# Moving the operand tiles of two expert layers to other bytes of their partitions, in a long convolution followed by two expert layers

## The chip, the cores and the metric

The kernel runs on one core of one Trainium2 chip. The metric is the device time in microseconds of one execution; the time before is the median of three. All rows below are from one profiled execution of the kernel before the change.

## The reference

Three stages follow one another: a gated long convolution done with Fourier transforms, then two expert layers (matrices 128 x 2048 and 2048 x 128), on 24,960 tokens of width 128.

```python
def _attn_ref(x, v, pos_emb, w1, w2):
    ...
    u = x * v
    ...
    y = np.fft.irfft(Uf * Hf[None, :, :], n=L, axis=1)[:, :S, :]
    return (x * y).astype(np.float32)

def _moe_ref(x, w_in, w_out):
    h = x @ w_in
    g = h * np.cos(h)
    return (g @ w_out).astype(np.float32)

def _moe2_ref(x, w_in, w_out):
    h = x @ w_in
    relu6 = np.clip(h + 3.0, 0.0, 6.0)
    g = h * relu6 / 6.0
    return (g @ w_out).astype(np.float32)
```

## The kernel before, in words

Every engine's program is written out in a fixed order; no scheduler decides it. The convolution (function `conv_phase`) comes first. While it runs, the weights of both experts are decoded into SBUF (`decode`), each matrix as a pair of tiles of type fp32r: a high part (`w_hi`) and a low part (`w_lo`). The names in the profile are `wi` and `wo` for the in and out matrices of the first expert, `vi` and `vo` for those of the second.

Then `moe_phase` runs both experts over tiles of tokens: 49 tiles, of which the first and the last have 448 tokens and the others 512. A tile of the first expert is `xh` and `xl` (high and low part of the input; for the first tile of all `x0h` and `x0l`), of the second expert `x2h` and `x2l`. Each tile is worked through in 8 units. A unit has a front (L696) of six matmuls with 128 x 128 weights and 512 (or 448) moving columns, two blocks of three: high weights with high input, high weights with low input, low weights with high input. It writes PSUM tile `ha` (first expert, in the main part) or `hb` (second expert). ScalarE, VectorE and GpSimd then make the gated value and its split `hi` and `lo`. A unit's back (L764) is six more matmuls: `hi` twice on the high weights, `hi` twice on the low weights, `lo` twice on the high weights, into PSUM tile `acc`.

In the main part one pass of the loop over `p` issues on TensorE, in this order, the front of a unit of the first expert (`ha<-xh,wi`), the back of an earlier one (`acc<-hi,wo`), the front of a unit of the second expert (`hb<-x2h,vi`, 12 units behind), and the back of an earlier one of those (`acc<-hi,vo`): 24 matmuls. Passes 0 to 11 hold units of the first expert alone, the last 12 those of the second alone, and 380 passes in between hold both. Each matmul has its own weight load (PEld in the profile), which runs while the matmul before it is still streaming.

**Where the tiles lie.** The tile pools are stacked in each partition from byte 0 up, each tile padded to a multiple of 32 bytes. Sizes are fixed, so the first byte of each tile follows from adding them up. What matters here is that byte modulo 256. All tiles of a pool of `moe_phase` are multiples of 2048 bytes, every weight block is 512 bytes from the next, the low part of a weight tile 8192 from the high part, and the second half of `hi` and `lo` 2048 from the first, so that one number holds for all matmuls of a kind. Before the change:

| tiles | first byte modulo 256 |
|---|---|
| `wi`, `wo` (weights, first expert) | 128 |
| `vi` (weights in, second expert) | 160 |
| `vo` (weights out, second expert) | 192 |
| `x0h`, `x0l` (moving, first tile) | 128 |
| `xh`, `xl`, `x2h`, `x2l`, `hi`, `lo` (moving) | 224 |

Three sizes make the odd places: tile `x0` has 4 x 113 x 4 = 1808 bytes (16 over a multiple of 256, padded to 32), and `vi` and `vo` share their memory with the filter tiles `h0` and `h1` of the convolution, 36 x 114 x 4 = 16,416 bytes each (32 over). Below, "offset" is the first byte of the moving tile less that of the weights, modulo 256: 96 with `wi` and `wo`, 64 with `vi`, 32 with `vo`, 0 for `x0h` and `x0l` with `wi`.

Of the kernel before, what the change touches and what calls it, by code (L numbers as in the profile page):

```python
# [9 lines left out]
FP32 = mybir.dt.float32  # L10
F32R = mybir.dt.float32r
# [12 lines left out]
N1, N2 = 111, 113  # L24
# [4 lines left out]
MP = 2 * M2  # L29
# [4 lines left out]
DFF = 2048  # L34
KFF = DFF // 128
TOK = B * S
TT = 512
XW = 4 * N2
TILES = [(TT + TOK % TT) // 2] + [TT] * (TOK // TT - 1) + [(TT + TOK % TT) // 2]
TWO_PI = 2.0 * np.pi  # L40

# [2 lines left out]
def kernel(  # L44
# [19 lines left out]
    nc = tc.nc  # L64
    dram = ctx.enter_context(tc.tile_pool(name="dram", bufs=1, space=DRAM))
    wp = ctx.enter_context(tc.tile_pool(name="wp", bufs=1))
    scr = dram.tile([D, B, NP1 * N2], FP32, name="scr")
# [5 lines left out]
    hq = ctx.enter_context(tc.tile_pool(name="hq", bufs=1))  # L73

    def weights(e, nm):
        if (nm, e) not in w_hi:
            if e == 0:
                t = wp.tile([128, 2, DFF], F32R, name=f"w{nm}")
            else:
                t = hq.tile([128, 2, DFF], F32R, tag=f"h{'io'.index(nm)}", name=f"v{nm}")  # L80
            w_hi[nm, e], w_lo[nm, e] = t[:, 0, :], t[:, 1, :]
        return w_hi[nm, e], w_lo[nm, e]

# [23 lines left out]
    def decode(task, st, pool, lane):  # L107
        e, nm, c = task
        lo, hi = st[:, :, 0], st[:, :, 1]
        ex = pool.tile([128, DC], INT32, tag=f"wex{lane}", name="wex")  # L110
        mh = pool.tile([128, DC], INT32, tag=f"wmh{lane}", name="wmh")
        m = mh.bitcast(FP32)
        wh, wl = (w[:, c:c + DC] for w in weights(e, nm))
        nc.vector.tensor_scalar(ex, hi, 9, 0x3FFFFF, op0=ALU.logical_shift_right, op1=ALU.bitwise_and)
        nc.vector.tensor_scalar(mh, hi, 0x1FF, None, op0=ALU.bitwise_and)
        yield
        nc.scalar.activation(out=ex, in_=ex, func=ACTF.Relu, bias=b_exp, scale=-1.0)
        nc.scalar.activation(out=ex, in_=ex, func=ACTF.Relu, bias=b_max, scale=-(2.0 ** 12))
        nc.scalar.activation(out=m, in_=mh, func=ACTF.Copy, scale=2.0 ** -20)
        yield  # L120
        nc.vector.scalar_tensor_tensor(
            out=ex, in0=hi, scalar=-0x80000000, in1=ex, op0=ALU.bitwise_and, op1=ALU.bitwise_or
        )
        yield
        nc.scalar.copy(wh, ex.bitcast(FP32))
        nc.vector.scalar_tensor_tensor(
            out=m, in0=lo.bitcast(UINT32), scalar=2.0 ** -52, in1=m, op0=ALU.mult, op1=ALU.add
        )
        yield
        nc.vector.tensor_scalar(ex, ex, -0x800000, None, op0=ALU.bitwise_and)  # L130
        yield
        nc.gpsimd.tensor_tensor(out=wl, in0=m, in1=ex.bitcast(FP32), op=ALU.mult)
# [17 lines left out]
    x0_t = {}  # L150
    x0h = wp.tile([128, TILES[0]], F32R, name="x0h")
    x0l = wp.tile([128, TILES[0]], F32R, name="x0l")

    def conv_phase(cctx):
# [408 lines left out]
            mk_y(i)  # L563

        n = NG
        x0 = x0_t[0] = wp.tile([128, XW], FP32, name="x0")

        def x_tile(shape, name):
            return p_x.tile(shape, FP32, tag="x", name=name)
# [8 lines left out]
        v = ps_v.tile([NP1, 2, 512], FP32, tag="v", name="v")  # L578
# [9 lines left out]
        def pass_on(i, z, eng, cs_=range(CH)):  # L588
            for c in cs_:
                d = i * CH + c  # L590
                eng.dma_start(
                    out=x0[d:d + 1, :].rearrange("c (n m) -> c n m", m=N2), in_=z[:XW // N2, 0, c, :N2]
                )

        s1i_3(0)
# [13 lines left out]
        w_of(n - 1, 0, wp_)  # L609
        fin_of(n - 1, 0, z1[:, 0], nc.vector, wp_[:, 1])  # L610
        e = (n - 3) * CH
        nc.sync.dma_start(out=x0[:e], in_=scr[:e, 0, :XW])
        pass_on(n - 3, z3, nc.sync)
        pass_on(n - 2, z2, nc.sync, (0,))
        pass_on(n - 1, z1, nc.sync)
        s1i_3(1)
        s2i(n - 2, 1)
# [10 lines left out]
                store_of(i, b, z[:, b])  # L628

    def moe_phase(mctx):  # L630
        x_p = mctx.enter_context(tc.tile_pool(name="x_p", bufs=3))
        x2_p = mctx.enter_context(tc.tile_pool(name="x2_p", bufs=2))
        o_p = mctx.enter_context(tc.tile_pool(name="o_p", bufs=2))
# [6 lines left out]
        nc.scalar.activation(out=dummy, in_=bias3, func=ACTF.Sin)  # L640
        NT = len(TILES)
        starts = [sum(TILES[:t]) for t in range(NT)]
        xs = {}
# [3 lines left out]
        def n_of(t):  # L647
            return TILES[t]

        def load_x(t):  # L650
            if t >= NT:
                return
            n = n_of(t)
            if t == 0 and n <= XW and _runs(0, n) == [[0, 0, n]]:
                xf[t] = x0_t[t]
# [135 lines left out]
        for p in range(P2 + 3):  # L791
            if p < P1:
                t, u = divmod(p, NU)
# [36 lines left out]
    with tc.manual_schedule():  # L830
        nc.gpsimd.memset(b_exp, 1151.0 * 2.0 ** 11 - 1.0)
        nc.gpsimd.memset(b_max, 255.0 * 2.0 ** 23 - 2.0 ** 12)
        nc.gpsimd.memset(b_one, 1.0)
        nc.gpsimd.memset(bias3, 3.0)
        nc.gpsimd.memset(biaspi, float(np.pi / 2))
        nc.gpsimd.memset(biasq, 0.25)
        with ExitStack() as cctx:
            conv_phase(cctx)
        with ExitStack() as mctx:
            moe_phase(mctx)  # L840
# [8 lines left out]
def _runs(a, n):  # L849
    valid = np.flatnonzero(_order()[1].reshape(-1) < S)  # L850
    runs = []
    for j in range(a, a + n):
        b, p = j // S, int(valid[j % S])
        if runs and runs[-1][0] == b and runs[-1][1] + runs[-1][2] == p:
            runs[-1][2] += 1
        else:
            runs.append([b, p, 1])
    return runs
# [78 lines left out]
```

## Time and profile before

| | us |
|---|---|
| time before, median of 3 (lowest, highest) | 2731.19 (2731.03, 2733.28) |
| span of the profiled execution | 2729.6 |
| convolution, to the last of its matmuls | about 529 |
| start of the experts, with waits, to 591 us | about 62 |
| the 376 passes in which both experts have fronts and backs, from 591 us | about 2096 |
| last passes and store | about 42 |
| PE busy in the span | 2712.7 (99%) |
| DVE, ACT, POOL busy | 2343.9, 2184.7, 2410.3 (86%, 80%, 88%) |

The profiled execution's own time is its span of 2729.6 us, 1.6 us under the median: what lies around the span is within the spread of the times. Matmuls in the profile overlap (the recorded length of one is near 0.39 us while the next starts 0.23 us later), so a busy PE tells little, and what counts is the distance from one matmul's start to the next one's, called the pitch below. A merged row of a timeline ends its stretch where the last matmul of the row ends, so pitches are taken from the starts of rows and the counts between them.

### The profile page before, as it was taken

What the parts mean: (1) busy time and instruction counts of PE and PEld (TensorE: products, weight loads), DVE (VectorE), ACT (ScalarE), POOL (GpSimd) and SP (SyncE); (2) the same over time, 40 slices, a digit from 0 to 9 for tenths busy, and PEclk for the clock granted to TensorE, in tenths of its full rate; (3) what the DMA queues carried; (4) which work ended last, traced back from release to release, by engine and by line L of the source; (5) the groups of instructions that cost most, each with busy time, mean ns of one, the idle gap of its engine ahead of it and who ended that gap; (6) DMA issues with size and microseconds to landing.
All of it is one profiled execution on the core that took longest, in us unless ns stands there. A gap on an engine that the chain in (4) does not pass through costs nothing.

```text
span 2729.6 us, 45722 instructions
## 1 busy us (share of the span) xinstructions
PE 2712.7 (99%) x16362; PEld 2151.5 (79%) x16362; DVE 2343.9 (86%) x3188; ACT 2184.7 (80%) x3140; POOL 2410.3 (88%) x1321
## 2 busy tenths in 40 slices
PE   9999999999999999999999999999999999999999
PEld 6777777678888888888888888888888888888888
DVE  7999998788888888888888888888888888888887
ACT  5666665588888888888888888888888888888885
POOL 6999998689888888888888989888988888888987
PEclk9999999999999999999999999999999999999999
DMA  4334333200000000000000000000000000000000
GB/s 122 100 105 106 105 98 83 64 5 16 8 16 8 16 9 16 9 16 9 16 8 16 13 11 16 9 16 9 16 9 16 8 16 8 16 9 16 8 8 12
DMA packets 88312, 79.86 MB, mean 29 GB/s; under 512 B 57028, under 2 KB 78870, under 8 KB 88086
## 3 DMA queue, kind: packets, MB, share of 16 engines
q1 hardware_dynamic: 87790, 76.80, 10.4%
q8 instruction: 132, 2.16, 0.3%
q14 instruction: 94, 0.77, 0.1%
q10 hardware_dynamic: 296, 0.13, 0.0%
HBM read 51.15 MB, written 25.74 MB: 28 GB/s over the span
## 4 chain that ended last, share of the span: by engine, by line
PE 98%; ACT 1%; DVE 1%; POOL 0%; issue 0%; DMA 0%; SPq 0%; ACTq 0%; DVEq 0%
PE acc L764 40%; PE hb L696 20%; PE ha L696 19%; PE ap L277 5%; PE v L277 3%; PE xp L277 3%; PE bp L277 3%; PE xh L277 2%; PE ap L276 1%; PE rp L329 0%; PE hps L342 0%; PE bp L276 0%; ACT r L716 0%; POOL lo L729 0%; ACT k L706 0%
## 5 line engine op out<-in xcount | busy, mean ns | idle before, releaser
L754 POOL TENSOR_TENSOR lo<-g,hi 128x1024 fp32r<-128x1024 f32 (+1 forms) x390 | 939.2, 2408 | 237.7 <-PE ha L696 157.1
L729 POOL TENSOR_TENSOR lo<-g,hi 128x1024 fp32r<-128x1024 f32 (+1 forms) x392 | 942.6, 2405 | 3.5 <-ACT hi L724 2.8
L706 ACT ACTIVATE k<-ha,biasq 128x512 int32<-128x512 f32 (+1 forms) x768 | 509.0, 689 | 293.7 <-PE ha L696 293.6
L717 DVE TENSOR_TENSOR g<-ha,r 128x512 f32<-128x512 f32 (+1 forms) x768 | 500.0, 690 | 283.8 <-ACT r L716 283.7
L696 PE MATMUL hb<-x2h,vi 128*128 128x512 f32 (+1 forms) x1564 | 549.8, 392 | 0.0
L696 PE MATMUL ha<-xh,wi 128*128 128x512 f32 (+1 forms) x1524 | 535.1, 391 | 3.1 <-DVE g L717 3.1
L716 ACT ACTIVATE r<-r,biaspi 128x512 f32<-128x512 f32 (+1 forms) x776 | 520.0, 719 | 0.4 <-DVE r L707 0.4
L707 DVE SCALAR_TENSOR_TENSOR r<-k,ha 128x512 f32<-128x512 int32 (+1 forms) x768 | 488.9, 677 | 2.9 <-ACT k L706 2.3
L737 DVE SCALAR_TENSOR_TENSOR g<-q,hb 128x1024 f32<-128x1024 f32 (+1 forms) x391 | 472.7, 1209 | 8.3 <-ACT q L736 8.2
L751 DVE SCALAR_TENSOR_TENSOR hi<-q,hb 128x1024 fp32r<-128x1024 f32 (+1 forms) x390 | 470.1, 1205 | 0.0
L736 ACT ACTIVATE q<-hb,bias 128x1024 f32<-128x1024 f32 (+1 forms) x391 | 435.3, 1113 | 20.8 <-PE hb L696 17.4
L764 PE MATMUL acc<-hi,wo 128*128 128x512 f32 (+1 forms) x1568 | 428.6, 395 | 0.0
L764 PE MATMUL acc<-hi,vo 128*128 128x512 f32 (+1 forms) x1568 | 428.2, 395 | 0.0
L724 ACT CAST hi<-g 128x1024 fp32r<-128x1024 f32 (+1 forms) x385 | 399.7, 1038 | 0.0
L764 PEld LDWEIGHTS acc<-hi,wo 128*128 128x128 f32 x1568 | 295.5, 188 | 71.5
L696 PEld LDWEIGHTS hb<-x2h,vi 128*128 128x128 f32 x1564 | 293.9, 188 | 69.0 <-issue 0.4
L764 PEld LDWEIGHTS acc<-hi,vo 128*128 128x128 f32 x1568 | 294.3, 188 | 68.5
L696 PEld LDWEIGHTS ha<-xh,wi 128*128 128x128 f32 x1524 | 286.0, 188 | 71.0 <-issue 2.8
L696 PE MATMUL hb<-x2l,vi 128*128 128x512 f32 (+1 forms) x782 | 306.5, 392 | 0.0
L696 PE MATMUL ha<-xl,wi 128*128 128x512 f32 (+1 forms) x762 | 303.7, 399 | 0.0
L764 PE MATMUL acc<-lo,wo 128*128 128x512 f32 (+1 forms) x784 | 248.0, 397 | 0.5 <-POOL lo L729 0.2
L764 PE MATMUL acc<-lo,vo 128*128 128x512 f32 (+1 forms) x784 | 245.8, 394 | 0.0
(155 smaller groups left out, 4084.1 us busy)
## 6 DMA issues: line engine op xcount, KB each, us to landing
x<-in_x_dram SPq DMA_DIRECT2D x64, 199.5 KB
v<-in_v_dram SPq DMA_DIRECT2D x64, 199.5 KB
scr<-z SPq DMA_DIRECT2D x128, 98.9 KB
out_dram<-o SPq DMA_DIRECT2D x47, 256.0 KB
xf<-scr SPq DMA_DIRECT2D x17, 256.0 KB
wst<-in_wi_dram SPq DMA_DIRECT2D x8, 512.0 KB
wst<-in_wo_dram SPq DMA_DIRECT2D x8, 512.0 KB
pt<-in_post_dram SPq DMA_DIRECT2D x14, 224.0 KB
```

Of the source, the lines that this page charges most:

```text
L277: nc.tensor.matmul(out=out[OD:m], lhsT=lhsT[:, OD:m], rhs=rhs if rhs2 is None else rhs2)
L696: nc.tensor.matmul(out=hs[c][:, 0, :n], lhsT=w["i", e][:, sl], rhs=r[:, :n], start=(k == 0), stop=(k == 2))
L706: nc.scalar.activation(out=k[:, c, :n], in_=h, func=ACTF.Identity, bias=biasq, scale=1.0 / TWO_PI)
L707: nc.vector.scalar_tensor_tensor(out=un.r[:, c, :n], in0=k[:, c, :n], scalar=-TWO_PI, in1=h, op0=ALU.mult, op1=ALU.add)
L716: nc.scalar.activation(out=rc, in_=rc, func=ACTF.Sin, bias=biaspi, scale=1.0)
L717: nc.vector.tensor_tensor(out=un.g[:, c, :n], in0=h, in1=rc, op=ALU.mult)
L729: nc.gpsimd.tensor_tensor(out=un.lo[:, :, :n], in0=un.g[:, :, :n], in1=un.hi[:, :, :n], op=ALU.subtract)
L736: nc.scalar.activation(out=un.r[:, c, :n], in_=h, func=ACTF.Relu, bias=bias3, scale=1.0)
L737: nc.vector.scalar_tensor_tensor(out=un.g[:, c, :n], in0=un.r[:, c, :n], scalar=6.0, in1=h, op0=ALU.min, op1=ALU.mult)
L751: nc.vector.scalar_tensor_tensor(out=un.hi[:, c, :n], in0=un.r[:, c, :n], scalar=6.0, in1=h, op0=ALU.min, op1=ALU.mult)
L754: nc.gpsimd.tensor_tensor(out=un.lo[:, :, :n], in0=un.g[:, :, :n], in1=un.hi[:, :, :n], op=ALU.subtract)
L764: nc.tensor.matmul(out=acc[e][:, :n], lhsT=w["o", e][:, sl], rhs=r[:, c, :n], start=(u == 0 and c == 0 and k == 0), stop=(u == KFF // 2 - ...
```

## The change

The sizes of five tiles are rounded up to a multiple of 256 bytes, and a tile of 64 bytes that nothing uses is put ahead of the pools of `moe_phase`. All weights then start at byte 128 modulo 256, and all moving tiles from the second on at byte 192: the offset is 64 in every front and back. `x0h` and `x0l` stay at 128, offset 0. Every tile of the convolution that lies above `x0` moves up as well, those above `h0` and `h1` all by the same 672 bytes, so that the offsets among them stay what they were. No instruction is added, removed, resized or put elsewhere in its engine's order, and every wait waits for the same semaphore and count as before.

```diff
+LINE = 64
+HB = -(-max(36 * MP, 2 * DFF) // LINE) * LINE
+XB = -(-XW // LINE) * LINE
...
-                t = hq.tile([128, 2, DFF], F32R, tag=f"h{'io'.index(nm)}", name=f"v{nm}")
+                t = hq.tile([128, HB], F32R, tag=f"h{'io'.index(nm)}", name=f"v{nm}")[:, :2 * DFF]
+                t = t.rearrange("p (z f) -> p z f", f=DFF)
...
-        x0 = x0_t[0] = wp.tile([128, XW], FP32, name="x0")
+        x0 = x0_t[0] = wp.tile([128, XB], FP32, name="x0")
...
-                    out=x0[d:d + 1, :].rearrange("c (n m) -> c n m", m=N2), in_=z[:XW // N2, 0, c, :N2]
+                    out=x0[d:d + 1, :XW].rearrange("c (n m) -> c n m", m=N2), in_=z[:XW // N2, 0, c, :N2]
...
-        nc.sync.dma_start(out=x0[:e], in_=scr[:e, 0, :XW])
+        nc.sync.dma_start(out=x0[:e, :XW], in_=scr[:e, 0, :XW])
...
     def moe_phase(mctx):
+        step = mctx.enter_context(tc.tile_pool(name="step", bufs=1))
+        step.tile([128, LINE // 4], FP32, name="step")
```

## Rows read from the trace of the kernel before

**Rows 1.** The page: span, busy time, and the chain that ended last.
```profile
span 2729.6 us, 45722 instructions
PE 2712.7 (99%) x16362; PEld 2151.5 (79%) x16362; DVE 2343.9 (86%) x3188; ACT 2184.7 (80%) x3140; POOL 2410.3 (88%) x1321
...
PE 98%; ACT 1%; DVE 1%; POOL 0%; issue 0%; DMA 0%; SPq 0%; ACTq 0%; DVEq 0%
PE acc L764 40%; PE hb L696 20%; PE ha L696 19%; PE ap L277 5%; PE v L277 3%; PE xp L277 3%; PE bp L277 3%; PE xh L277 2%; PE ap L276 1%; PE rp L329 0%; PE hps L342 0%; PE bp L276 0%; ACT r L716 0%; POOL lo L729 0%; ACT k L706 0%
```

**Rows 2.** Busy time of each engine by stage: busy us and count, granted clock.
```profile
core 0: us, PE busy (x) PEld busy (x) DVE busy (x) ACT busy (x) POOL busy (x), PEclk, DMA share, GB/s
0.00:528.70 528.70, 524.48 (x6936) 382.14 (x6938) 454.48 (x796) 323.09 (x655) 463.93 (x474) 1.00 0.37 98
528.70:591.00 62.30, 53.14 (x225) 42.56 (x222) 45.97 (x60) 50.09 (x68) 53.10 (x36) 0.95 0.11 30
...
633.80:2644.90 2011.10, 2011.10 (x8641) 1621.38 (x8640) 1739.96 (x2206) 1721.68 (x2295) 1788.85 (x766) 1.00 0.04 12
2644.90:2687.40 42.50, 42.50 (x194) 36.06 (x193) 36.98 (x50) 35.25 (x52) 36.61 (x17) 1.00 0.02 7
2687.40:2729.60 42.20, 38.71 (x181) 33.33 (x179) 29.64 (x30) 17.09 (x21) 30.42 (x15) 0.99 0.03 13
```

**Rows 3.** Timeline of the weight loads in one front and back.
```profile
642.17 0.19 PEld L696 LDWEIGHTS hb<-x2l,vi 128*128 128x128 f32 x1
```

**Rows 4.** Timeline of PE in one pass of the main part.
```profile
639.37 0.39 PE L696 MATMUL ha<-xh,wi 128*128 128x512 f32 x1
639.60 0.40 PE L696 MATMUL ha<-xl,wi 128*128 128x512 f32 x1
639.84 0.62 PE L696 MATMUL ha<-xh,wi 128*128 128x512 f32 x2
...
642.17 0.40 PE L696 MATMUL hb<-x2h,vi 128*128 128x512 f32 x1
642.41 0.39 PE L696 MATMUL hb<-x2l,vi 128*128 128x512 f32 x1
642.64 0.62 PE L696 MATMUL hb<-x2h,vi 128*128 128x512 f32 x2
643.10 0.39 PE L696 MATMUL hb<-x2l,vi 128*128 128x512 f32 x1
643.32 0.39 PE L696 MATMUL hb<-x2h,vi 128*128 128x512 f32 x1
643.55 1.10 PE L764 MATMUL acc<-hi,vo 128*128 128x512 f32 x4
```

**Rows 5.** Chain that ended last, in time order: start, us, what; first passes.
```profile
617.52 1.41 PE ha L696 x6
618.93 1.40 PE acc L764 x6
620.33 1.37 PE hb L696 x6
621.70 1.24 PE acc L764 x6
...
639.53 1.39 PE ha L696 x6
640.93 1.40 PE acc L764 x6
642.33 1.39 PE hb L696 x6
643.72 1.40 PE acc L764 x6
```

**Rows 6.** Timeline of PE while the granted clock was 0.50, and the clock.
```profile
575.25:577.30 2.05, 2.05 (x6) 1.63 (x5) 2.00 (x3) 2.02 (x4) 2.05 (x2) 0.50 0.01 4
575.63 1.91 PE L764 MATMUL acc<-hi,wo 128*128 128x512 f32 x4
577.34 1.00 PE L764 MATMUL acc<-lo,wo 128*128 128x512 f32 x2
```

**Rows 7.** Timeline of PE with 448 columns: convolution, first tile, last tile.
```profile
206.58 0.54 PE L277 MATMUL xp<-at,cs 121*49 121x448 f32 x1
206.96 0.54 PE L277 MATMUL xp<-at,cs 121*49 121x448 f32 x1
...
536.70 0.36 PE L696 MATMUL hb<-x0h,wi 128*128 128x448 f32 x1
538.92 0.37 PE L696 MATMUL hb<-x0h,wi 128*128 128x448 f32 x1
...
2714.91 0.37 PE L696 MATMUL hb<-x2h,vi 128*128 128x448 f32 x1
2716.12 0.98 PE L764 MATMUL acc<-hi,vo 128*128 128x448 f32 x4
2717.35 0.36 PE L696 MATMUL hb<-x2h,vi 128*128 128x448 f32 x1
```

**Rows 8.** Timeline of DVE, and of PE, around the release of `ha`.
```profile
1503.59 1.30 DVE L717 TENSOR_TENSOR g<-ha,r 128x512 f32<-128x512 f32 x2 [0.23 <-ACT r L716]
...
1505.77 0.62 PE L696 MATMUL ha<-xh,wi 128*128 128x512 f32 x2
```

## The prediction

> **What bounds the kernel now.** First the page: the chain that ended last lies 98% on PE, and four fifths of it are the fronts and backs of the two experts, L696 and L764 [rows 1]. Then the busy times by stage: from 633.80 to 2644.90 us PE has no gap at all, at a granted clock of 1.00 (the level of 2.4 GHz), while DVE, ACT and POOL are busy for 1740, 1722 and 1789 of 2011.10 us [rows 2]. These are 360 passes of 24 matmuls, 8640 (the row counts 8640 loads), so a pass takes 5.586 us and the mean pitch is 232.8 ns. The time is set by how fast PE goes from one matmul to the next, and by nothing that PE waits for.
>
> Now what such a pitch should be. 512 columns at 2.4 GHz are 213.3 ns, so each of these matmuls loses about 19 ns. At the lower level nothing is lost: where the granted clock was 0.50, four matmuls took 1.71 us from start to start, 427 ns each, and 512 columns at 1.2 GHz are 426.7 [rows 6]. The convolution loses little at 2.4 GHz: its matmuls of 448 columns, which go through their columns twice, have a pitch of 0.38 us, 190 ns or less for once, against 186.7 worked out and against 202 to 205 ns for the experts' matmuls of 448 columns [rows 7]. So some 18 ns per matmul are lost in the experts alone and at the full clock alone. Under every matmul the weight load for the next one is running: the load of `hb<-x2l,vi` starts at 642.17, as the matmul before it does [rows 3, 4].
>
> **Does the loss depend on where the tiles lie?** Within a pass the pitches are uneven, though all 24 matmuls have the same shape: the front of the second expert has steps of 0.24, 0.23, 0.46 for two, 0.22 and 0.23 us [rows 4]. Sorted by the offset of the weights that load meanwhile:
>
> - Offset 96 (`wi`, `wo`): six take 1.39 to 1.41 us, 232 to 235 ns each [rows 5].
> - Offset 32 (`vo`), 512 columns: 1.40 us for six, 233 ns [rows 5].
> - Offset 64 (`vi`): 1.39 in the main part, but 1.37 in the first passes, 228 ns [rows 5]. In the main part it begins with the slow step of 0.24 and ends with faster ones, 0.91 us for the last four [rows 4]: what a matmul costs depends also on the steps before it, and six matmuls are few to settle in. In the passes around 620 us it has settled from its first step on.
> - With 448 columns the same: offset 64 takes 1.21 us for six (201.7 ns) and offset 32 takes 1.23 (205 ns), in neighbouring rows; offset 0 (`x0h` on `wi`) takes 2.22 us for eleven, 201.8 ns [rows 7].
>
> So offsets 0 and 64 are alike, 32 and 96 are alike, and the first pair is 3 to 5 ns cheaper per matmul. As far as these rows go, whole multiples of 64 bytes are good and odd multiples of 32 are bad.
>
> The Trainium skill speaks against any such effect: its page "TensorE: Matmul & The Clock Gate", in the section on what each phase is for, says that TensorE reads the moving operand and the weights through two independent SBUF ports, so that loading the next weights takes no read bandwidth from the running matmul. By that rule the change is worth nothing and the time stays at 2731; the pitches that differ by weight tile do not fit it.
>
> **The change part by part.** No instruction, size, order or wait changes, so there is no added work to price. Four things move.
>
> *Fronts and backs with 512 columns.* All now stand at offset 64, with no step from one offset to another within a pass or between passes. I price each six at the settled 1.37 us of the vi front [rows 5]. A pass becomes 4 x 1.37 = 5.48 us, 0.106 less than 5.586, and 360 passes give -38 us. The row is rounded to 0.01: half a hundredth on each six is 7 us on 360 passes. Bounds: from above the worst six with the same shape, 1.41 (a loss, below); from below the rate of the convolution, at most 190 ns for 448 columns, thus 215 ns or so for 512 and 1.29 for six. I stay with 1.37, since it is the one row with the very offset, columns and type.
>
> *Passes with 448 columns in one expert.* There are 8 at each end, the last 8 taking 42.50 us [rows 2]. A six at 448 gains about 0.02 where it had offset 32 or 96 [rows 7] and one at 512 gains 0.026 as above, some 0.1 a pass: -1.5 us. The last twelve passes hold `vo` backs beside `vi` fronts: -0.3. The start of the experts has 9 us without a matmul in 62 [rows 2] and offset 0 in its fronts, and I count nothing there.
>
> *The convolution.* Its tiles move together, so their offsets stay. Its pitch is at the bound already, so there is nothing to gain. If the place alone, without the offset, brought in the experts' loss of 8%, its 524 us of PE would cost 42 more; no row suggests it, and I take 0.
>
> *The elementwise engines.* They read and write the moved tiles, and no pitch of PE follows them. A faster PE asks more of them: per pass POOL has 1788.85 / 360 = 4.97 us of work, DVE 4.83, ACT 4.78, against a new 5.48 [rows 2]. The tightest loop that I see is PSUM tile `ha`: its last reader on DVE ends at 1504.89, and the first matmul that overwrites this half is the second of the pair that starts at 1505.77, thus at 1506.00 [rows 8]. That leaves 1.1 us of cover, and a pass shorter by 0.1 uses a tenth of it. If the cover were gone, PE would wait and the gain would end where POOL's 4.97 stand, beyond my forecast.
>
> Sum: -38 - 1.5 - 0.3 = -40, with 2 us less because the 1.37 contains one step towards another offset, and because a row of 1.37 may stand for up to 1.375: I take -39. The profiled execution (span 2729.6) is 1.6 us under the median, so I take the difference off the median: 2731.2 - 39 = 2692.
>
> **Rivals.**
>
> *It doesn't settle.* The cheap run at 620 us may hang on the state that it was entered from, and the main part's vi front (1.39) may be what offset 64 gives on the whole. Then a pass is 4 x 1.39 = 5.56, 0.026 less, and 376 passes give -10: 2721; with 1.385, inside that row's rounding, 2714. For it: the slow first step of every vi front in the main part. Against it: by their last steps these fronts do 0.91 for four. Chance 0.14.
>
> *Nothing changes.* The uneven steps come from the order of the matmuls and not from the place of the weights, and the time stays at 2731. For it: fronts at offset 96 also show 1.39 in the main part. Against it: the rows with 448 columns, where the order is the same in both experts. Chance 0.08. (It is what the rule of the Trainium skill named above would give.)
>
> *Slower, by the place and not the offset.* The vi front is the only one of the 512-column rows in which both streams start at an odd multiple of 32 (160 and 224), and after the change both start at an even one (128 and 192). If that costs what the worst front costs, 1.41 for six, a pass takes 5.64: +0.054 x 360 = +19, so 2751. It decides from a mean six of about 1.400 on. Against it: `x0h` and `wi` both start at 128 and go at 201.8 ns, among the best with 448 columns [rows 7]. Chance 0.06, the convolution's 42 us included.
>
> *More than forecast.* If every step were the best single one, 0.225, a pass would be 5.40, and -0.186 x 360 = -67 gives 2664; at the convolution's rate it would be near 2580. A front that already has offset 64 shows neither. Chance 0.12, nearly all of it above 2660.
>
> **How the numbers follow.** The forecast (2684 to 2703 by its own rounding and transitions) has 0.60. With "doesn't settle" at 0.14 and half of "more" the range is 2668 to 2722, which leaves out no change, slower and the far end of more: 0.2. A change of 0.2%, 5.5 us, is about what a measurement of this kernel can tell from none; "doesn't settle" lies beyond it for all but 0.02. So faster 0.84, same 0.10, slower 0.06.
>
> **What would show it.** Right: in the main part the stage of 360 passes lasts about 1973 us instead of 2011.10, all four sixes of a pass read 1.37, PE still has no gap, the convolution's 528.7 us stay, and the durations of the elementwise operations stay. Wrong: sixes of 1.39 or 1.40 in spite of offset 64 everywhere (no settling, or no effect of the offset), a six over 1.40 (the place matters), or waits of PE on `g` or `lo` in the main part (an elementwise engine has become the bound).

## The result and the profile after

The changed kernel takes 2696.1 us (median of 4, 2695.94 to 2697.06), 0.9872 of the time before, with a 95% interval of 0.9858 to 0.9886. The forecast was 2692 in 2668 to 2722, faster. The profiled execution's span is 2694.4 us, 35.2 less than that of before.

Busy times by stage, of the changed kernel; columns as in [rows 2], which answers row by row, but for the third row here, the first passes with both experts; its row of before stands below:

```profile
0.00:528.70 528.70, 523.89 (x6928) 380.76 (x6930) 453.97 (x794) 322.38 (x654) 463.79 (x474) 1.00 0.37 98
528.70:591.26 62.56, 54.16 (x234) 43.02 (x233) 46.59 (x63) 51.08 (x69) 53.72 (x37) 0.95 0.11 31
591.26:633.37 42.11, 42.11 (x193) 36.01 (x192) 36.74 (x49) 37.42 (x52) 37.34 (x17) 1.00 0.04 13
633.37:2610.97 1977.60, 1977.60 (x8642) 1622.61 (x8640) 1739.63 (x2206) 1705.11 (x2296) 1782.97 (x766) 1.00 0.05 13
2610.97:2652.66 41.69, 41.69 (x193) 36.03 (x192) 36.82 (x50) 35.02 (x52) 36.52 (x17) 1.00 0.02 7
2652.66:2694.40 41.74, 38.27 (x181) 33.29 (x179) 29.60 (x30) 17.16 (x22) 30.57 (x15) 0.99 0.04 13
```

Before the change:

```profile
590.97:633.78 42.81, 42.81 (x193) 36.07 (x192) 36.82 (x49) 37.56 (x52) 37.41 (x17) 1.00 0.04 12
```

The 360 full passes take 1977.60 us instead of 2011.10: -33.5 of the 35.2. The 8 passes with 448 columns at each end give 0.7 and 0.8, the last twelve 0.5, and convolution and start of the experts together end 0.3 later. PE still has no gap in the passes. In time order the chain of the changed kernel reads, where [rows 5] had 1.39 and 1.40:

```profile
639.03 1.37 PE ha L702 x6
640.40 1.37 PE acc L770 x6
641.77 1.37 PE hb L702 x6
643.15 1.37 PE acc L770 x6
```

and the timeline of PE, where [rows 4] began the `vi` front with a step of 0.24 us:

```profile
641.61 0.39 PE L702 MATMUL hb<-x2h,vi 128*128 128x512 f32 x1
641.84 0.39 PE L702 MATMUL hb<-x2l,vi 128*128 128x512 f32 x1
642.07 0.62 PE L702 MATMUL hb<-x2h,vi 128*128 128x512 f32 x2
642.52 0.39 PE L702 MATMUL hb<-x2l,vi 128*128 128x512 f32 x1
642.75 0.39 PE L702 MATMUL hb<-x2h,vi 128*128 128x512 f32 x1
642.99 1.07 PE L770 MATMUL acc<-hi,vo 128*128 128x512 f32 x4
```

Every step is now 0.22 to 0.24. The starts in nanoseconds show one cycle of three, 226, 229 and 231 or 232, in all four sixes: 5493 or 5494 ns in each of the 361 passes with 512 columns alone. That is the run that the `vi` front showed around 620 us before the change.

### The profile page after: what moved, and what is told of

Its sections match the earlier page's. It is cut to its first block, busy times and chain, and to the rows that moved or that the text cites. A ratio compares the mean times of both kernels' runs of the same rounds, so it can differ in the third digit from the quotient of the medians.

```text
span 2694.4 us, 45722 instructions
## 1 busy us (share of the span) xinstructions
PE 2677.7 (99%) x16362; PEld 2151.7 (80%) x16362; DVE 2343.4 (87%) x3188; ACT 2168.2 (80%) x3140; POOL 2404.9 (89%) x1321
## 4 chain that ended last, share of the span: by engine, by line
PE 98%; POOL 1%; ACT 1%; DVE 1%; issue 0%; DMA 0%; ACTq 0%; DVEq 0%; POOLq 0%
PE acc L770 39%; PE hb L702 20%; PE ha L702 19%; PE ap L281 5%; PE v L281 3%; PE xp L281 3%; PE bp L281 3%; PE xh L281 2%; PE ap L280 1%; PE rp L333 1%; PE hps L346 0%; PE bp L280 0%; POOL lo L735 0%; ACT k L712 0%; ACT r L722 0%
## 5 line engine op out<-in xcount | busy, mean ns | idle before, releaser
L770 PE MATMUL acc<-hi,wo 128*128 128x512 f32 (+1 forms) x1568 | 420.1, 390 | 0.0
L770 PE MATMUL acc<-hi,vo 128*128 128x512 f32 (+1 forms) x1568 | 419.5, 389 | 0.0
```

Of the source, the lines that this page charges most:

```text
L770: nc.tensor.matmul(out=acc[e][:, :n], lhsT=w["o", e][:, sl], rhs=r[:, c, :n], start=(u == 0 and c == 0 and k == 0), stop=(u == KFF // 2 - ...
```

## The experiments

Each run edits the changed kernel, unless it says otherwise. "Offset" is still the moving tile's first byte less that of the weights, modulo 256.

**1. Many offsets, by extra matmuls.** Sets of 40 matmuls stand behind the twelve matmuls `busy<-wi` that the kernel issues ahead of the experts, with a narrow one ahead of each set. The granted clock was 1.00 over all sets. The added work counts in its time, 3460.92 us, so only the pitches are read.

```diff
+        wa, wb = w_hi["i", 0], w_hi["o", 0]
+        scan = [(0, k, 128, TT) for k in range(64)]
+        scan += [(0, k, m, TT) for m in (64, 32) for k in (0, 8, 16, 24)]
+        scan += [(j, j + 16, 128, TT) for j in (4, 8, 12)] + [(j, j + 24, 128, TT) for j in (4, 8, 12)]
+        scan += [(0, k, 128, 448) for k in (0, 8, 16, 24)]
+        for j, k, m, n in scan:
+            nc.tensor.matmul(out=busy[:32, :64], lhsT=wb[:, :32], rhs=wb[:, :64])
+            for _ in range(40):
+                nc.tensor.matmul(out=busy[:m, :n], lhsT=wa[:, j:j + m], rhs=wa[:, k:k + n])
```

> The changed kernel with 82 sets of 40 extra matmuls (128 x 128 weights unless said otherwise, 512 columns) behind the twelve that warm TensorE; they read two slices of the first expert's weights and write a PSUM tile that nothing reads. In a set all matmuls have one offset between moving slice and weights; sets step it by 4 bytes from 0 to 252. Theory A (the offset modulo 64 counts): the pitch repeats every 64 bytes, lowest at 0, 64, 128, 192 (about 227 to 229 ns) and high at 32, 96, 160, 224 (about 233). Theory B (64 itself counts): a lowest pitch near 64 alone. Theory C (only that the offset is the same everywhere counts): all sets alike, about 228.6. Loads of 64 and 32 columns: if the loss comes from the load that runs under a matmul, it falls from some 15 to 20 ns over 213.3 in proportion to the columns loaded; if it is a fixed cost of a matmul it stays. Sets that shift weights and moving slice together by 16, 32, 48 bytes: the same pitch if the offset alone counts, another if the place does.

Timeline of PE in that run, sets with offsets 0, 32, 64 and 100, each with the narrow matmul that ends it:

```profile
533.16 9.36 PE L802 MATMUL busy<-wi 128*128 128x512 f32 x40
542.36 0.19 PE L800 MATMUL busy<-wo 128*32 128x64 f32 x1
...
608.25 9.58 PE L802 MATMUL busy<-wi 128*128 128x512 f32 x40
617.66 0.19 PE L800 MATMUL busy<-wo 128*32 128x64 f32 x1
...
683.31 9.42 PE L802 MATMUL busy<-wi 128*128 128x512 f32 x40
692.57 0.19 PE L800 MATMUL busy<-wo 128*32 128x64 f32 x1
...
768.13 9.82 PE L802 MATMUL busy<-wi 128*128 128x512 f32 x40
777.79 0.19 PE L800 MATMUL busy<-wo 128*32 128x64 f32 x1
```

The 40 take 9.20, 9.41, 9.26 and 9.66 us. Without the first step of each set (some 0.31 us, behind the narrow matmul) and the steps until the set has settled, the mean distance of starts over the last 29 is:

```
offset (bytes)          0     32     64     96    128    160    192    224
pitch, 512 cols (ns)  226.7  233.4  228.8  233.4  232.3  234.2  233.2  233.4
lowest and highest of all 64 offsets: 226.7 (0, 28, 60, 108, 156, 252) and 240.0 (68, 100, 132, 180, 196, 228, 244)
weights of 64 columns 230.1  230.8  228.4  230.1
weights of 32 columns 231.6  233.3  231.6  233.3
448 moving columns    206.7  200.0  200.0  205.3
```

Theory A is wrong: 128 and 192 are multiples of 64 and cost about as much as 32. Theory C is wrong: a set has one offset and still pays 226.7 to 240. Theory B holds no better, as 0 beats 64. The loss does not shrink in proportion to the columns loaded: at offsets 32 and 96 a load of 64 columns costs about 3 ns less, but one of 32 columns no less, and at offset 0 the narrower load costs more. With 448 columns the order of the offsets is another one. The sets that shift weights and moving slice together show that the place can count besides the offset: offset 64 costs 226.7 ns with a shift of 16 or 48 bytes, against 228.8 with 0 or 32; offset 96 stays at 233.3 to 233.4.

**2. Offset 0 in the whole kernel.** The 64-byte tile is taken out, the rounded sizes stay.

```diff
-        step = mctx.enter_context(tc.tile_pool(name="step", bufs=1))
-        step.tile([128, LINE // 4], FP32, name="step")
```

> The changed kernel without the 64-byte tile: all moving tiles of the experts start where the weights do, modulo 256 (offset 0). Theory A (offset modulo 64): as the changed kernel or a little faster, sixes of 1.36 to 1.37 us, 2685 to 2697 us. Theory B (64 itself): slower than the changed kernel, sixes of 1.39 to 1.41, 2715 to 2745. Theory C (uniformity): 2696.

It takes 2677.39 us, 0.9801 of before (0.9787 to 0.9816), with sixes of 1.36. That is below what any of the three theories gave (2685 at the least), and it is the scan's price for offset 0: 24 x 226.7 ns are a pass of 5.440 us, which the trace shows. So the rounding of sizes alone gains 54 us, and the 64-byte tile then gives back 19 of them. It is the fastest kernel of this study.

**3. Offset 96.**

```diff
-        step.tile([128, LINE // 4], FP32, name="step")
+        step.tile([128, 3 * LINE // 8], FP32, name="step")
```

> The changed kernel with a tile of 96 bytes in place of 64: offset 96 in every front and back. Theory A (offset modulo 64): the gain is lost or more than lost; all sixes at the 1.40 of the wo backs before, a pass of 5.60 us, about 2735 us. Theory B: above 2715 as well. Theory C (uniformity alone): 2696, with sixes of 1.37.

2736.93 us, 1.0018 of before (1.0009 to 1.0028): one offset everywhere gains nothing if it is this one. Uniformity is not the cause. Theory A had this time too (2735), so this run alone does not tell it from a price for each offset; runs 1 and 10 do.

**4. Another place, the same offset.**

```diff
     dummy = wp.tile([128, 1], FP32, name="dummy")
+    wp.tile([128, 8], FP32, name="place")
```

> The changed kernel with a 32-byte tile ahead of all tiles of the experts: the offset stays 64 everywhere, but weights start at 160 and moving tiles at 224 modulo 256, as the second expert's front did before. Theories A, B and C (offset or uniformity): 2696, sixes of 1.37. Theory D (both streams have to start at a multiple of 64): the gain is lost wholly or in part, above 2710.

2696.35 us, 0.987 (0.9854 to 0.9886), as the changed kernel. Where both streams lie does not count, for this offset and a shift of 32 bytes.

Busy times over one and the same stretch show what a uniform offset costs, since PE has no gap in it; four of them: the changed kernel (64),

```profile
640.00:2600.00 1960.00, 1960.00 (x8565) 1608.16 (x8564) 1724.22 (x2187) 1690.66 (x2276) 1767.48 (x759) 1.00 0.05 12
```

offset 0,

```profile
640.00:2600.00 1960.00, 1960.00 (x8650) 1623.16 (x8649) 1742.07 (x2208) 1701.03 (x2299) 1778.70 (x766) 1.00 0.05 13
```

offset 96,

```profile
640.00:2600.00 1960.00, 1960.00 (x8402) 1576.75 (x8401) 1691.24 (x2145) 1676.47 (x2231) 1743.51 (x744) 1.00 0.05 12
```

and offset 68, run 8 below:

```profile
640.00:2600.00 1960.00, 1960.00 (x8168) 1568.03 (x8167) 1677.65 (x2085) 1634.50 (x2171) 1408.05 (x724) 1.00 0.04 12
```

The stretch divided by the count is the pitch: 228.8, 226.6, 233.3 and 240.0 ns, at a granted clock of 1.00 in all four. These are the prices of the first scan, to 0.1 ns.

**5. More sets: farther away, fewer columns, other reads.**

```diff
+        for k in (256, 264, 281, 512, 520, 537, 1024, 1032, 1049):
+            mm_set(40, wa[:, :128], wa[:, k:k + TT])
+        for n in (504, 496, 480, 448, 384, 320):
+            for k in (0, 17):
+                mm_set(40, wa[:, :128], wa[:, k:k + n])
+        for k in (0, 17):
+            mm_set(40, wa[:, :128], wa[:, k:k + 1].to_broadcast([128, TT]))
+        for k in (0, 17, 34):
+            mm_set(40, wh[:, :128], wh[:, k:k + TT])
+        for k in (0, 17):
+            mm_set(40, wf[:, :128], wf[:, k:k + TT])
...
+            for r in range(4):
+                for _ in range(10):
+                    nc.tensor.matmul(out=busy, lhsT=wa[:, 32:160] if r % 2 else wa[:, 15:143], rhs=wa[:, 32:32 + TT])
```

(`wh` and `wf` are the same bytes read as bf16 and as fp32.)

> More sets of extra matmuls, as in the first scan. Theory P (phase: each load and the stream beside it meet at an offset modulo 256 bytes, and the loss is columns + 32 to columns + 64 cycles of 2.4 GHz): moving slices 1024, 2048 and 4096 bytes on (each also with 32 and 100 bytes more) cost what offsets 0, 32 and 100 cost in the first scan, 226.7, 233.4 and 240.0 ns. With fewer columns (504 to 320) no set goes below columns + 32 cycles. Moving slices that read one element 512 times: if the loss is a clash of places in SBUF, it changes and no longer depends on the offset, and if it is fixed it stays at 226.7 or more. bf16 slices of the same bytes: half the bytes for each column and another form of load, so about 214 to 216 ns if the loss comes from the fp32r load, the same 226.7 and more if it comes from the matmul. Blocks of ten that change the weights' place between offset 68 (240 ns) and 0 (226.7): each step is at the price of the weights that load under it if that sets the loss; at the price of the weights in use if not.

Moving slices 1024, 2048 and 4096 bytes on cost 226.7 or 226.8 ns, 32 more 233.3, 100 more 240.0: the pattern repeats with 256 bytes. Timeline of PE, sets with one element read 512 times (offsets 0 and 68), then the first with bf16:

```profile
716.26 8.99 PE L801 MATMUL busy<-wi 128*128 128x512 f32 x40
725.08 0.19 PE L799 MATMUL busy<-wo 128*32 128x64 f32 x1
725.11 8.99 PE L801 MATMUL busy<-wi 128*128 128x512 f32 x40
733.93 0.19 PE L799 MATMUL busy<-wo 128*32 128x64 f32 x1
733.97 8.81 PE L801 MATMUL busy<-wi 128*128 128x512 bf16 x40
```

Settled, the one-element sets are at 218.7 ns with either offset, bf16 at 215.8 to 216.7 with three, and fp32 at 429.2 per record, two runs over the columns, with both. So of what was tried only fp32r streams that walk through SBUF pay for the offset. The tiles of the convolution's matmuls are of type fp32, so the fp32 sets also bear on why the loss that the prediction found was "in the experts alone": 429.2 ns for two runs over 512 columns are 214.6 for one. With fewer columns no set goes below columns + 32 cycles, as expected: at offset 0, 504 columns give 226.7 ns (columns + 40), 480 give 216.6 (+ 40), 384 give 173.3 (+ 32). But 448 columns at offset 0 now settle at 202.7 ns, where the first scan had 206.7: for that number of columns the sets before decide as well. The blocks of ten with offset 68 went at about 233 ns and not at the expected 240 (run 9 has 233.4 for this offset when the weights are moved), and the blocks took 3 to 6 steps at each change; the first change away from 226.7 came one matmul before the new weights were in use, while they were loading, but one such place is not enough to rest on.

**6. The 64-byte tile alone, on the kernel before.**

```diff
     def moe_phase(mctx):
+        step = mctx.enter_context(tc.tile_pool(name="step", bufs=1))
+        step.tile([128, 16], FP32, name="step")
```

> The kernel before with the 64-byte tile ahead of the expert pools and none of the rounding of sizes: offsets 160 with wi and wo, 128 with vi, 96 with vo. Theory P with the first scan's prices (234.2, 232.3, 233.4): a pass of 24 at about 233.5, 5.60 us, 2731 to 2740 us, no gain. Rival (the 64-byte step is what gains): near 2696 to 2710.

2737.88 us, 1.0021 (1.0011 to 1.003): no gain, within the stated 2731 to 2740.

**7 and 8. Four bytes lower, four bytes higher.** All moving tiles of the experts are 256 bytes longer and are used from element K on, 15 or 17, with no 64-byte tile: offsets 60 and 68.

```diff
+        def mv(pool, z, name):
+            t = pool.tile([128, z * TT + LINE], F32R, tag=name, name=name)[:, K:K + z * TT]
+            return t.rearrange("p (z f) -> p z f", f=TT) if z > 1 else t
...
-            un.hi = g_p.tile([128, 2, TT], F32R, tag="hi", name="hi")
+            un.hi = mv(g_p, 2, "hi")
```

> The changed kernel with all moving tiles of the experts 4 bytes lower: offset 60 everywhere. Theory P: 226.7 ns per matmul as at offset 0, main pass 5.44 us, about 2677 us. Rival A (offset modulo 64, whole lines): an offset that is not a multiple of 64 loses, 2730 or more. If the elementwise engines pay for writing to tiles that do not start at a multiple of 32 bytes, their durations rise, and the time with them only if PE then waits.

> The changed kernel with all moving tiles of the experts 4 bytes higher: offset 68 everywhere. Theory P: 240.0 ns per matmul, a pass of 5.76 us, 0.267 more than the changed kernel's 5.493 in 376 passes, about 2796 us. Rival A: as any offset that is not a multiple of 64, about 2735. Rival C (uniformity): 2696.

Offset 68 takes 2796.82 us, 1.0235 (1.0218 to 1.0252), against 2796 expected: four bytes cost 101 us over the changed kernel, and its chain shows sixes of 1.44:

```profile
1500.33 1.44 PE ha L706 x6
1501.77 1.44 PE acc L774 x6
```

Offset 60 takes 2685.6 us, 0.983 (0.9815 to 0.9844): faster than the changed kernel, as expected, but by 10 us and not by 19. Its passes settle at 5.466 us, 227.8 ns per matmul and not 226.7:

```profile
640.00:2600.00 1960.00, 1960.00 (x8607) 1613.91 (x8606) 1733.21 (x2198) 1694.03 (x2287) 1767.88 (x763) 1.00 0.05 13
```

Weights (128) and moving tiles (188) start at the same bytes modulo 256 as in the scan's set with offset 60, so the difference is not one of place. The elementwise engines do not pay for the odd starts: `hi` on VectorE takes 1211 ns against 1210, `lo` on GpSimd 2413 against 2417 at offset 0.

**9. The weights are moved instead.** As run 1, with the moving slice fixed and the weights stepped by 4 bytes.

```diff
+        for j in range(64):
+            nc.tensor.matmul(out=busy[:32, :64], lhsT=wb[:, :32], rhs=wb[:, :64])
+            for _ in range(40):
+                nc.tensor.matmul(out=busy, lhsT=wa[:, j:j + 128], rhs=wa[:, 64:64 + TT])
```

> Sets of extra matmuls as in the first scan, but now the moving slice stays at byte 256 of the tile and the weights are stepped by 4 bytes, so that the offset runs from 256 down to 4 with the moving place fixed. Theory P (the offset between the two alone sets the settled pitch): each offset costs what it did in the first scan within 1 ns (0: 226.7; 100, 132, 228: 240; 96, 224: 233.4). Rival (the place of either counts as well): several offsets differ by over 2 ns, as offset 64 did between 228.8 and 226.7 in the sets that shifted both by 16 bytes. The last eight sets have weights 2048 bytes on at offsets 0, 100, 32 and 64: the same pitch in each pair if the pattern repeats every 256 bytes.

```
offset (bytes)             0     32     64     96    128    160    192    224    60     68    100    132
run 1, moving stepped    226.7  233.4  228.8  233.4  232.3  234.2  233.2  233.4  226.7  240.0  240.0  240.0
run 9, weights stepped   226.7  233.2  229.0  233.5  232.3  234.2  233.2  233.4  233.4  233.4  226.7  231.7
```

On multiples of 32 bytes the two agree within 0.2 ns, so there the offset alone counts for 512 columns. Off that grid they differ by up to 13 ns, and the place of the weights counts as well. Only 19 of the 64 offsets agree within 1 ns, so theory P as stated holds on the grid alone.

The last eight sets, of 60 matmuls, agree in each pair within 0.2 ns: 226.7, 235.5, 233.4 and 229.0 ns for offsets 0, 100, 32 and 64, so 2048 bytes more change nothing. But offset 100 had settled at 240.0 in run 1, with the very same two slices. Here its steps repeat as 236, 237, 230, 233, 238, 240 and 236 ns, within 1 ns; there each is 240. The steps behind the narrow matmul differ already (230, 233, 237, 240 here, 233, 234, 238, 240 there), which suggests, but does not show, that what ran before a set decides which cycle it settles in. Either way a price from off the grid need not carry over to a whole kernel: that of offset 60 did not (run 7), that of 68 did (run 8).

**10. Offset 128 in the whole kernel.**

```diff
-        step.tile([128, LINE // 4], FP32, name="step")
+        step.tile([128, LINE // 2], FP32, name="step")
```

> The changed kernel with a tile of 128 bytes in place of 64: offset 128 everywhere. By the first scan's price (232.3 ns) a pass of 5.58 us and about 2727 us. Rival A (whole multiples of 64 are alike, the reading of the prediction): 2680 to 2697 us.

2728.75 us, 0.9992 (0.9982 to 1.0001), against 2727 by the scan. The reading "multiples of 64 are good" is refuted in the kernel too. Its steps settle in a cycle of seven, as in the scan: 241, 232, 231, 232, 228, 230 and 233 ns, within 1 ns. Seven does not divide 24, so the passes differ, from 5570 to 5586 ns, and the sixes read 1.39 or 1.40:

```profile
1502.40 1.40 PE hb L702 x6
1503.79 1.40 PE acc L770 x6
1505.19 1.40 PE ha L702 x6
1506.59 1.40 PE acc L770 x6
1507.98 1.40 PE hb L702 x6
1509.38 1.39 PE acc L770 x6
```

Over the stretch used above the mean pitch is 232.3 ns:

```profile
640.00:2600.00 1960.00, 1960.00 (x8436) 1588.97 (x8435) 1699.58 (x2154) 1678.78 (x2241) 1743.95 (x748) 1.00 0.05 12
```

## Why the prediction was right, and where it was not

**The bound was right.** PE has no gap in the passes before and after, the elementwise engines do the same work in less time, and the whole gain is a shorter pitch.

**The main term was right in kind and 5 us too large.** It priced each six at the 1.37 us of the `vi` front, rounded, and gave -38 with 7 us for the rounding. The settled six is 1977.60 / 1440 = 1.3733 us, which gives -33.5, within that bound. Its condition, that uniform offset 64 settles at once, held: the `vi` front's run around 620 us became the run of all four sixes. By the settled prices of offsets 96, 64 and 32 a pass of the kernel before would take 5.574 us (an estimate from run 1), and it took 5.586, while the changed kernel takes 5.493. So by this estimate about 0.08 of the 0.09 us gained in a pass come from the cheaper offset, and the rest from having no steps from one offset to another.

**The small terms** were -1.5 and -0.3 in the forecast and -1.5 and -0.5 in the trace; the convolution with the start of the experts came out 0.3 later against 0. The sum itself has a slip: -38 - 1.5 - 0.3 with 2 us less is -37.8, thus 2693, and the forecast took -39 and 2692. The 2 us were meant for the transition and the rounding; the rounding alone needed 4 to 5.

**The reading of the offsets was wrong.** "Whole multiples of 64 bytes are good and odd multiples of 32 are bad" came from four offsets of the trace. Offsets 128 and 192 go against it (runs 1, 9 and 10), and part of its support was not what it seemed: with 448 columns the scan has offset 32 at 200.0 and 0 at 206.7, so rows with 448 columns say nothing on 512. The forecast did not suffer, since its price came from the one row with the very offset, columns and type; the rule would have allowed 128 as well, which gains 2 or 3 us (run 10, not clear of noise) and not 39. What stands in place of the rule: for fp32r with 512 columns, one offset throughout and starts that are multiples of 32 bytes, the settled pitch followed the offset modulo 256 in every set and kernel tried. It is to be measured and not guessed. With 448 columns one and the same offset, 0, settled at 206.7 ns in run 1 and at 202.7 in run 5, so no such table holds there.

**The rivals.** Not settling, no change and slower by the place all fell: sixes of 1.37 throughout, and run 4 with another place gave the same time. "More than forecast" did not happen at this offset, but it is what offset 0 does: 226.7 ns and 2677.39 us, near the 5.40 us a pass that the best single step gave as a bound (5.440).

**The rule of the Trainium skill** (page "TensorE: Matmul & The Clock Gate", on what each phase is for), that loading the next weights takes no read bandwidth from the running matmul, agrees with the bf16 and fp32 sets of run 5, which keep their pitch within 1 ns at the three and two offsets tried. It does not describe the fp32r matmuls of this kernel, whose pitch goes from 226.7 to 240.0 ns with the places of weights and moving data.

**What stays open is the mechanism.** When the stream reads one element the pitch falls to 218.7, with either offset; that, and that it otherwise depends on the offset, speak for a clash of the two streams in SBUF. Two things speak against a mere count of clashes: a load of a quarter of the columns did not cost less (231.6 and 233.3 ns), and the fp32 sets, which read the same bytes with a load of the same recorded 0.19 us under each record of 429.2 ns, are only 2.5 ns over 426.7, at offset 68 as at 0. A run of fp32r matmuls without weight loads was not tried, so it is not shown that the load that runs under a matmul is what the stream meets.

## What to carry to other kernels

Where a matmul engine has no gaps, compare the pitch with columns over clock before calling it full: some 19 ns of 232.8 were lost here without a single wait in the trace. For fp32r, put all weights and all moving tiles at fixed places modulo 256 bytes, measure a handful of offsets on the 32-byte grid with some tens of extra matmuls each, and take the best: it was 0, worth 54 us of 2731 here, while 64 gave 35 and 96 cost 5. A price from such a set held in the kernel for the four offsets of that grid that were tried in both (0, 64, 96 and 128). With other columns, or off the grid, the set and the kernel can differ, and the kernel itself has to be timed.

## What was not expected of the hardware

GpSimd's subtraction `lo<-g,hi` became faster when `hi` and `lo` started 68 bytes, instead of 60, over a multiple of 256 plus 128. Costliest groups of GpSimd, 1360 to 1920 us, offset 60:

```profile
L764 POOL TENSOR_TENSOR lo<-g,hi 128x1024 fp32r<-128x1024 f32 x103 | 248.5, 2413 | 55.6 <-PE ha L706 51.7 <-DVE hi L761 2.9
```

and offset 68:

```profile
L764 POOL TENSOR_TENSOR lo<-g,hi 128x1024 fp32r<-128x1024 f32 x97 | 194.6, 2006 | 120.3 <-DVE hi L761 118.0 <-PE ha L706 2.3
```

2413 ns became 2006, with the operation, the shape and the types the same. In the same stretch of all other whole kernels, where `hi` and `lo` start at 0, 32, 128, 188, 192 or 224 modulo 256, both of its lines took 2408 to 2426 ns; only the start at 196 is faster, and there `xl<-xf,xh` is too (1096 ns against 1292 to 1307). Since GpSimd does not set the time here it brought nothing. The runs do not separate the start from the slower pace of PE in run 8.

The settled pitches of the scans are often whole multiples of 16 cycles of 2.4 GHz: 226.7 is 544 cycles, 233.3 is 560, 240.0 is 576, 200.0 is 480, 173.3 is 416. Nothing in the trace before had suggested steps of that size.
